# One more SBUF buffer, fewer early reloads, paired loads and split tiles at the turn between two passes of a channel-attention kernel

## The chip, the cores and the metric

The kernel runs on one core of one Trainium2 chip. The metric is the device time of one execution in microseconds (us). Two executions (one of an experiment, one of the kernel before) took over 770 us; they were left out as slow, from medians too. The experiments e9, e10 and e11 ran on another chip than the other experiments; their ratios are against the kernel before on that chip (757.38 us there).

## The reference

```python
def setup_inputs():                       # H = W = C = 384, k = 1, everything bf16
    return {"x": normal(1, 384, 384, 384) * 0.05, "w1d": normal(1) * 0.05}

def reference(x, w1d):
    g = x.sum over all pixels / (H * W)    # one mean per channel
    s = sigmoid(g * w1d[0])                # k = 1: no neighbours
    return x * s                           # per channel
```

No output can be written until every input has been read, because `s` needs the mean over all pixels. The input has 113.25 MB in 72 tiles. It does not fit in SBUF, the memory on the chip, where a build with 18 tiles was refused (see "The change"), so most of it must be read twice.

## The kernel before

In this kernel PE does the matmuls (2.77 us for a tile in the trace), DVE the multiplies (3.35 us) and ACT the sigmoid (0.58 us); SP issues the loads of the tiles and ACT their stores.

The input is cut into 72 tiles of 128 partitions x 12 KB (1.57 MB). In the first pass, SP loads every tile into a ring of 16 buffers, and PE multiplies it by a matrix of ones into one PSUM accumulator, which gives the channel sums in all partitions. ACT applies the sigmoid. In the second pass, DVE multiplies tiles by `s` in place and ACT's queue stores them. The last tiles are still in SBUF and need no second load. Each other tile is reloaded into a buffer whose store is done. `NS` tiles of those still in SBUF are given up on purpose: their buffers take reloads before any store is done, so these reloads run while PE, ACT and DVE finish the first pass.

```python
TILE_BYTES_TARGET = 12 * 1024
MAX_BUF_BYTES = 192 * 1024
MAX_BUFS = 16
NS_TARGET = 3
...
    resident = list(range(NT - NBUF, NT - NS))                            # kept: 13 tiles
    reload = list(range(0, NT - NBUF)) + list(range(NT - NS, NT))         # read twice: 59 tiles
    vorder = resident + reload
...                                                                       # sync engine
            for i in range(NT):                                           # first pass
                b = i % NBUF
                j = i // NBUF
                if j > 0:
                    sync.wait_ge(pe_sems[b], j)
                sync.dma_start(bufs[b][:], x_tiles[i]).then_inc(in_sems[b], 16)
            for i in reload:                                              # second pass
                b = p2_buf[i]
                sync.wait_ge(pe_sems[b], cnt1[b])
                if load_wait_out[i] > 0:                                  # 0 for the first NS of them
                    sync.wait_ge(out_sems[b], load_wait_out[i])
                sync.dma_start(bufs[b][:], x_tiles[i]).then_inc(in_sems[b], 16)
```

## Time and profile before

| | kernel before |
|---|---|
| median, lowest, highest of its first 6 runs | 757.33, 755.71, 758.18 us |
| span of the profiled run | 753.9 us |
| tiles moved: first loads + reloads + stores | 72 + 59 + 72 = 203 |
| bytes moved | 319.48 MB |
| busy: PE, DVE | 27%, 32% |

The first view is from the profile page of the kernel before: the span in 40 equal slices, with the busy share in tenths of PE, DVE and the DMA engines, and then the rate in GB/s.

```profile
PE   5777777777777740000000000000000000000000
...
DVE  0000000000000029998445354444535444453300
...
DMA  8999999999999999999999999999999999999998
GB/s 341 425 426 425 423 426 424 426 422 426 424 425 423 426 395 424 429 429 430 431 430 430 428 432 430 428 429 431 431 429 430 430 431 429 429 429 431 432 430 382
```

DMA is at 90% or more in nearly every slice. PE works in the first 15 slices, DVE in the rest, and neither is full for long. So the DMA engines bound the kernel. The table of DMA queues (packets, MB, share of the time of 16 engines) says what they carry; q1 is the load queue and q10 the store queue:

```profile
q1 hardware_dynamic: 18864, 206.05, 64.8%
q10 hardware_dynamic: 10368, 113.25, 35.3%
```

The next view gives the DMA issues by group: how many, KB each, median us from issue to landing.

```profile
buf<-in_x_dram SPq DMA_DIRECT2D x131, 1536.0 KB, 27.0
out_dram<-buf ACTq DMA_DIRECT2D x72, 1536.0 KB, 71.0
```

A store lands 71 us after its issue (the median).

This is the timeline of the kernel before (start us, length us, engine, line, operation, output<-inputs, count, and in brackets the idle time before it):

```profile
268.47 8.56 SPq L152 DMA_DIRECT2D buf<-in_x_dram  x3
...
273.90 2.77 PE L186 MATMUL acc<-buf,ones_mat 128*128 128x384 bf16 x16 [1.76 <-DMA buf<-in_x_dram]
276.78 0.58 ACT L123 ACTIVATE s_bc<-acc,w_scaled 128x384 bf16<-128x384 f32 x1 [274.54 <-PE acc L186]
277.39 6.63 DVE L172 TENSOR_TENSOR buf<-buf,s_bc 128x6144 bf16<-128x6144 bf16 x2 [266.04 <-ACT s_bc L123]
280.78 0.38 ACTq L133 DMA_DIRECT2D out_dram<-buf  x1
```

The last tile is seen by PE at 273.90. The first store is issued at 280.78, 6.88 us later: 16 matmuls, the sigmoid, one multiply of 3.35 us. The early reloads were issued from 268.47 on. Now the DMA engines in chosen windows of the same run (window, length, busy time of PE, PEld (PE's weight loads), DVE, ACT, POOL with counts, then the granted TensorE clock, DMA share, GB/s):

```profile
10.00:255.00 245.00, 183.20 (x1053) 97.67 (x1052) 0.15 (x1) 0.00 (x0) 0.00 (x0) 1.00 1.01 425
270.00:273.00 3.00, 2.14 (x14) 1.07 (x11) 0.00 (x0) 0.00 (x0) 0.00 (x0) 1.00 0.95 385
273.00:276.00 3.00, 2.10 (x13) 1.28 (x14) 0.00 (x0) 0.00 (x0) 0.00 (x0) 1.00 0.99 385
276.00:279.00 3.00, 0.68 (x5) 0.20 (x2) 1.61 (x1) 0.58 (x1) 0.00 (x0) 1.00 1.02 369
279.00:282.00 3.00, 0.00 (x0) 0.00 (x0) 3.00 (x2) 0.00 (x0) 0.00 (x0) 0.91 0.93 373
380.00:680.00 300.00, 0.00 (x0) 0.00 (x0) 137.70 (x41) 0.00 (x0) 0.00 (x0) 0.50 1.01 430
```

The rate is 425 GB/s in the first pass and 430 in the steady second pass, so a tile costs about 3.7 us anywhere. Around the turn the rate dips, but DMA is hardly idle (shares of 0.93 to 1.02): three early reloads fill the turn.

### The profile page before, as it was taken

The page shows a single profiled execution, that of the slowest core. Times are in us where ns is not written, and L with a number is a line of the kernel's source. Part 1 is how long each engine was busy: PE and PEld are TensorE (multiplying, and loading weights), DVE is VectorE, ACT ScalarE, POOL GpSimd, SP SyncE. Part 2 cuts the span into 40 slices and gives each one's busy share as a digit, 9 for nine tenths or more (in the row PEclk, how much of TensorE's full clock was granted, in tenths as well). Part 3 has the DMA queues.
Part 4 walks back from the last instruction along what each step waited for, and adds up shares of the span by engine and source line. Part 5 has one row for each costly group of instructions (what it writes and reads, how often), then busy time and mean ns, then how long its engine had stood idle before and what let it go on. Part 6 is the DMA issues. An engine that isn't in the chain of part 4 may idle for free.

```text
span 753.9 us, 2681 instructions
## 1 busy us (share of the span) xinstructions
PE 201.7 (27%) x1152; PEld 107.5 (14%) x1152; DVE 240.2 (32%) x74; ACT 2.1 (0%) x3; POOL 1.0 (0%) x6
## 2 busy tenths in 40 slices
PE   5777777777777740000000000000000000000000
PEld 2343333343444420000000000000000000000000
DVE  0000000000000029998445354444535444453300
ACT  0000000000000000000000000000000000000000
POOL 0000000000000000000000000000000000000000
PEclk9999999999999995555555555555555555555555
DMA  8999999999999999999999999999999999999998
GB/s 341 425 426 425 423 426 424 426 422 426 424 425 423 426 395 424 429 429 430 431 430 430 428 432 430 428 429 431 431 429 430 430 431 429 429 429 431 432 430 382
DMA packets 29388, 319.48 MB, mean 424 GB/s; under 512 B 3392, under 2 KB 3392, under 8 KB 3392
## 3 DMA queue, kind: packets, MB, share of 16 engines
q1 hardware_dynamic: 18864, 206.05, 64.8%
q10 hardware_dynamic: 10368, 113.25, 35.3%
q8 instruction: 9, 0.15, 0.1%
q0 software_dynamic: 144, 0.00, 0.0%
q14 instruction: 3, 0.02, 0.0%
HBM read 206.05 MB, written 113.25 MB: 424 GB/s over the span
## 4 chain that ended last, share of the span: by engine, by line
another core or an unknown queue 40%; SPq 32%; DMA 14%; DVE 6%; issue 1%; PE 0%; ACT 0%; ACTq 0%
SPq L146 30%; DMA buf<-in_x_dram 8%; DMA out_dram<-buf 6%; DVE buf L172 6%; SPq L152 2%; PE acc L186 0%; SPq L151 0%; ACT s_bc L123 0%; ACTq L122 0%
## 5 line engine op out<-in xcount | busy, mean ns | idle before, releaser
L172 DVE TENSOR_TENSOR buf<-buf,s_bc 128x6144 bf16<-128x6144 bf16 x72 | 239.8, 3356 | 457.0 <-ACT s_bc L123 266.0
L186 PE MATMUL acc<-buf,ones_mat 128*128 128x384 bf16 x1152 | 201.7, 329 | 74.9 <-DMA buf<-in_x_dram 74.9
L186 PEld LDWEIGHTS acc<-buf,ones_mat 128*128 128x128 bf16 x1152 | 107.5, 98 | 168.8 <-DMA buf<-in_x_dram 94.6
L158 DVE TENSOR_SCALAR w_scaled<-w_f 128x1 f32<-128x1 f32 x1 | 0.2, 154 | 10.2 <-DMA w_f<-in_w1d_dram 10.2
L123 ACT ACTIVATE s_bc<-acc,w_scaled 128x384 bf16<-128x384 f32 x1 | 0.6, 581 | 274.5 <-PE acc L186 274.5
L118 ACT ACT_TABLE_LOAD x1 | 1.3, 1283 | 0.7 <-PEq L208 0.7
L112 POOL DMA_DIRECT2D w_f<-in_w1d_dram x1 | 0.7, 652 | 0.8 <-POOLq L208 0.8
L156 DVE MEMSET ones_mat<- 128x128 bf16 x1 | 0.2, 165 | 0.8 <-PEq L208 0.8
L118 ACT ACTIVATE warm<-warm 128x1 f32<-128x1 f32 x1 | 0.2, 203 | 0.0
L113 POOL MEMSET warm<- 128x1 f32 x1 | 0.1, 118 | 0.0
L208 POOL MEMSET const-uint8-127<- 128x1 uint8 x1 | 0.1, 101 | 0.0
L208 POOL MEMSET const-float32-0.0<- 128x1 f32 x1 | 0.1, 98 | 0.2 <-issue 0.2
L208 POOL MEMSET const-float32-1.0<- 128x1 f32 x1 | 0.1, 98 | 0.0
L208 POOL MEMSET const-bfloat16-1.0<- 128x1 bf16 x1 | 0.1, 98 | 0.0
## 6 DMA issues: line engine op xcount, KB each, us to landing
buf<-in_x_dram SPq DMA_DIRECT2D x131, 1536.0 KB, 27.0
out_dram<-buf ACTq DMA_DIRECT2D x72, 1536.0 KB, 71.0
w_f<-in_w1d_dram POOLq DMA_DIRECT2D x1, 0.5 KB, 10.0
```

The source lines that it names most:

```text
L112: gpsimd.dma_start(w_f32[:], w_bcast_src).then_inc(w_sem, 16)
L113: gpsimd.memset(warm[:, 0:1], 0.0).then_inc(warm_sem, 1)
L118: scalar.activation(warm[:, 1:2], warm[:, 0:1], mybir.ActivationFunctionType.Sigmoid)
L123: scalar.activation(s_bc[:], acc[:, :C], mybir.ActivationFunctionType.Sigmoid, scale=w_scaled[:, 0:1],).then_inc(s_sem, 1)
L146: sync.dma_start(bufs[b][:], x_tiles[i]).then_inc(in_sems[b], 16)
L152: sync.dma_start(bufs[b][:], x_tiles[i]).then_inc(in_sems[b], 16)
L156: vector.memset(ones_mat[:], 1.0).then_inc(ones_sem, 1)
L158: vector.tensor_scalar_mul(w_scaled[:], w_f32[:], inv_hw).then_inc(wsc_sem, 1)
L172: vector.tensor_tensor(bv, bv, s_b, mybir.AluOpType.mult).then_inc(vec_sems[b], 1)
L186: ins = tensor.matmul(acc[:, :C], ones_mat[:], bufs[b][:, t * C : (t + 1) * C], start=first, stop=last,)
L208: nc = _bacc.Bacc("TRN2", target_bir_lowering=False, num_devices=1)
```

## The change

It aims to move fewer bytes and to shorten the turn. It has four parts.

1. 17 buffers (204 KB per partition) instead of 16, in one array, so one tile more stays in SBUF. A version with 18 (216 KB) failed to build.
2. `NS` from 3 to 1. Together with part 1, reloads fall from 59 to 56.
3. The first pass loads pairs of neighbouring tiles with one DMA. The DRAM layout puts the two tiles side by side in a partition, so a run has 24 KB.
4. The last load comes in four quarters, each with its own semaphore, and the first six resident tiles are multiplied and stored in halves.

```diff
-MAX_BUF_BYTES = 192 * 1024
-MAX_BUFS = 16
-NS_TARGET = 3
+MAX_BUF_BYTES = 204 * 1024
+MAX_BUFS = 32
+NS_TARGET = 1
+GROUP = 2
...
+    RS = NT - MG - NS
+    recycled = list(range(RS, RS + NS))
+    resident = [i for i in range(NT - NBUF, NT) if i not in recycled]
+    reload = list(range(0, NT - NBUF)) + recycled
...
-    x_tiles = x.flatten_outer_dims().rearrange("(n p t) c -> n p (t c)", p=P, t=T)
+    x_mt = x.flatten_outer_dims().rearrange("(n p t) c -> n p (t c)", p=P, t=MG * T)
...                                                     # grouping of the first loads
+            i % MG == 0
+            and g < MG
+            and i + g < NT - 2 * MG
+            and (i + g) % NBUF == (i % NBUF) + g
...
+    HALF = 6
+    split = set(resident[:HALF])
...                                                     # sync engine, the last load
+                if gi == NT - 1:
+                    F4 = FD // LQ                       # LQ = 4
+                    for q in range(LQ):
+                        sync.dma_start(
+                            slot(s0)[:, q * F4 : (q + 1) * F4],
+                            dram_tiles(x_mt, gi, 1)[:, q * F4 : (q + 1) * F4],
+                        ).then_inc(last_sems[q], 16)
+                    continue
+                sync.dma_start(slot(s0, g), dram_tiles(x_mt, gi, g)).then_inc(
+                    in_sems[s0], 16
+                )
...                                                     # vector engine (stores are split the same way)
+                if i in split:
+                    for h in range(2):
+                        ...
+                        vector.tensor_tensor(
+                            bh, bh, s_h, mybir.AluOpType.mult
+                        ).then_inc(vec_sems[b], 1)
+                    continue
```

More of the change, by code (lines that the diff above doesn't have):

```diff
@@ L38, in bass_standalone__channel_attn_eca__vision_kernel @@
     assert C <= 512, "channel count must fit one PSUM bank"
+    MG = GROUP if (rows_pp % (GROUP * T) == 0 and NT >= GROUP) else 1
     NBUF = max(1, min(MAX_BUFS, NT, MAX_BUF_BYTES // tile_pp_bytes))
-    NS = 0 if NT <= NBUF else min(NS_TARGET, NBUF)
-    resident = list(range(NT - NBUF, NT - NS))
-    reload = list(range(0, NT - NBUF)) + list(range(NT - NS, NT))
+    NS = 0 if NT <= NBUF else min(NS_TARGET, NBUF - MG)
+    RS = NT - MG - NS
+    if RS < NT - NBUF:
+        RS = NT - NBUF
+    recycled = list(range(RS, RS + NS))
+    resident = [i for i in range(NT - NBUF, NT) if i not in recycled]
+    reload = list(range(0, NT - NBUF)) + recycled
     assert sorted(resident + reload) == list(range(NT))
@@ L47, in bass_standalone__channel_attn_eca__vision_kernel, with dram_tiles @@
     inv_hw = 1.0 / float(H * W)
-    x_tiles = x.flatten_outer_dims().rearrange("(n p t) c -> n p (t c)", p=P, t=T)
-    o_tiles = out.flatten_outer_dims().rearrange("(n p t) c -> n p (t c)", p=P, t=T)
+    x_mt = x.flatten_outer_dims().rearrange("(n p t) c -> n p (t c)", p=P, t=MG * T)
+    o_mt = out.flatten_outer_dims().rearrange("(n p t) c -> n p (t c)", p=P, t=MG * T)
+    def dram_tiles(view, i, g):
+        n, q = divmod(i, MG)
+        assert q + g <= MG
+        return view[n][:, q * FD : (q + g) * FD]
     w_bcast_src = bass.AP(w1d.tensor, w1d.offset, [[0, P], [1, 1]])
+    arena = nc.alloc_sbuf_tensor("arena", [P, NBUF * FD], x.dtype)
     ones_mat = nc.alloc_sbuf_tensor("ones_mat", [P, P], x.dtype)
@@ L63, in bass_standalone__channel_attn_eca__vision_kernel @@
     s_sem = nc.alloc_semaphore("s_sem")
-    bufs = []
+    LQ = 4
+    last_sems = [nc.alloc_semaphore(f"last_sem{q}") for q in range(LQ)]
     in_sems, pe_sems, vec_sems, out_sems = [], [], [], []
     for b in range(NBUF):
-        bufs.append(nc.alloc_sbuf_tensor(f"buf{b}", [P, FD], x.dtype))
         in_sems.append(nc.alloc_semaphore(f"in_sem{b}"))
@@ L71, in bass_standalone__channel_attn_eca__vision_kernel, with slot @@
         out_sems.append(nc.alloc_semaphore(f"out_sem{b}"))
-    cnt1 = [len(range(b, NT, NBUF)) for b in range(NBUF)]
-    buf_of_last = {i: i % NBUF for i in range(NT - NBUF, NT)}
-    p2_buf = {}
+    def slot(b, n=1):
+        return arena[:, b * FD : (b + n) * FD]
+    groups = []
+    i = 0
+    while i < NT:
+        g = 1
+        while (
+            i % MG == 0
+            and g < MG
+            and i + g < NT - 2 * MG
+            and (i + g) % NBUF == (i % NBUF) + g
+        ):
+            g += 1
+        groups.append((i, g))
+        i += g
@@ new lines, in bass_standalone__channel_attn_eca__vision_kernel @@
+    cnt1 = [len(range(b, NT, NBUF)) for b in range(NBUF)]
+    p1_wait = {}
+    dma_cnt = [0] * NBUF
+    p1_loads = []
+    uses1 = [0] * NBUF
+    for gi, g in groups:
+        s0 = gi % NBUF
+        waits = []
+        for q in range(g):
+            s = s0 + q
+            if uses1[s] > 0:
+                waits.append((s, uses1[s]))
+            uses1[s] += 1
+        if gi != NT - 1:
+            dma_cnt[s0] += 1
+        for q in range(g):
+            p1_wait[gi + q] = (s0, 16 * dma_cnt[s0])
+        p1_loads.append((waits, s0, gi, g))
@@ L76, in bass_standalone__channel_attn_eca__vision_kernel @@
+    slot_of_tail = {i: i % NBUF for i in range(NT - NBUF, NT)}
+    p2_slot = {}
     for i in resident:
-        p2_buf[i] = buf_of_last[i]
+        p2_slot[i] = slot_of_tail[i]
     for m, i in enumerate(reload):
         if m < NS:
-            p2_buf[i] = buf_of_last[NT - NS + m]
+            p2_slot[i] = slot_of_tail[recycled[m]]
         else:
-            p2_buf[i] = p2_buf[vorder[m - NS]]
-    n_loads = list(cnt1)
+            p2_slot[i] = p2_slot[vorder[m - NS]]
+    proc_index = {}
     n_proc = [0] * NBUF
-    load_wait_out = {}
@@ L86, in bass_standalone__channel_attn_eca__vision_kernel @@
-    vec_wait = {}
-    store_wait_vec = {}
-    proc_index = {}
     for i in vorder:
-        b = p2_buf[i]
+        b = p2_slot[i]
         proc_index[i] = n_proc[b]
         n_proc[b] += 1
-    load_wait_in_value = {}
-    for m, i in enumerate(reload):
-        b = p2_buf[i]
-        n_loads[b] += 1
-        load_wait_in_value[i] = 16 * n_loads[b]
-        load_wait_out[i] = 16 * proc_index[i]
-    for i in vorder:
-        b = p2_buf[i]
-        if i in load_wait_in_value:
-            vec_wait[i] = ("in", load_wait_in_value[i])
-        else:
-            vec_wait[i] = ("pe", cnt1[b])
-        store_wait_vec[i] = proc_index[i] + 1
@@ L106, in bass_standalone__channel_attn_eca__vision_kernel @@
-    total_stores = list(n_proc)
+    vec_wait = {}
+    load_wait_out = {}
+    for i in reload:
+        b = p2_slot[i]
+        dma_cnt[b] += 1
+        vec_wait[i] = ("in", 16 * dma_cnt[b])
+        load_wait_out[i] = 16 * proc_index[i]
+    for i in resident:
+        vec_wait[i] = ("pe", cnt1[p2_slot[i]])
+    HALF = 6
+    split = set(resident[:HALF])
+    xtra = [0] * NBUF
+    for i in split:
+        assert proc_index[i] == 0
+        xtra[p2_slot[i]] = 1
+    store_wait_vec = {i: proc_index[i] + 1 + xtra[p2_slot[i]] for i in vorder}
@@ L108, in bass_standalone__channel_attn_eca__vision_kernel @@
+    for i in reload:
+        if proc_index[i] > 0:
+            load_wait_out[i] += 16 * xtra[p2_slot[i]]
+    F2 = FD // 2
     with nc.Block() as block:
@@ L121, in _ @@
             scalar.wait_ge(wsc_sem, 1)
-            scalar.wait_ge(pe_sems[(NT - 1) % NBUF], cnt1[(NT - 1) % NBUF])
+            last_slot = (NT - 1) % NBUF
+            scalar.wait_ge(pe_sems[last_slot], cnt1[last_slot])
             scalar.activation(
@@ L130, in _ @@
             for i in vorder:
-                b = p2_buf[i]
+                b = p2_slot[i]
+                if i in split:
+                    for h in range(2):
+                        scalar.wait_ge(vec_sems[b], h + 1)
+                        scalar.dma_start(
+                            dram_tiles(o_mt, i, 1)[:, h * F2 : (h + 1) * F2],
+                            slot(b)[:, h * F2 : (h + 1) * F2],
+                        ).then_inc(out_sems[b], 16)
+                    n_st[b] += 2
+                    continue
                 scalar.wait_ge(vec_sems[b], store_wait_vec[i])
-                scalar.dma_start(o_tiles[i], bufs[b][:]).then_inc(out_sems[b], 16)
+                scalar.dma_start(dram_tiles(o_mt, i, 1), slot(b)).then_inc(
+                    out_sems[b], 16
+                )
                 n_st[b] += 1
@@ L140, in _ @@
         def _(sync):
-            for i in range(NT):
-                b = i % NBUF
-                j = i // NBUF
-                if j > 0:
-                    sync.wait_ge(pe_sems[b], j)
-                sync.dma_start(bufs[b][:], x_tiles[i]).then_inc(in_sems[b], 16)
+            for waits, s0, gi, g in p1_loads:
+                for s, val in waits:
+                    sync.wait_ge(pe_sems[s], val)
+                if gi == NT - 1:
[8 more added lines that the diff above has]
+                    in_sems[s0], 16
+                )
             for i in reload:
-                b = p2_buf[i]
+                b = p2_slot[i]
                 sync.wait_ge(pe_sems[b], cnt1[b])
@@ L151, in _ @@
                     sync.wait_ge(out_sems[b], load_wait_out[i])
-                sync.dma_start(bufs[b][:], x_tiles[i]).then_inc(in_sems[b], 16)
+                sync.dma_start(slot(b), dram_tiles(x_mt, i, 1)).then_inc(
+                    in_sems[b], 16
+                )
         @block.vector
@@ L161, in _ @@
             for i in vorder:
-                b = p2_buf[i]
+                b = p2_slot[i]
                 if first:
@@ L170, in _ @@
                     vector.wait_ge(pe_sems[b], val)
-                bv = bufs[b][:].rearrange("p (t c) -> p t c", t=T)
+                if i in split:
+                    s_h = s_bc[:].unsqueeze(1).broadcast_to([P, T // 2, C])
+                    for h in range(2):
+                        bh = slot(b)[:, h * F2 : (h + 1) * F2].rearrange(
+                            "p (t c) -> p t c", t=T // 2
+                        )
+                        vector.tensor_tensor(
+                            bh, bh, s_h, mybir.AluOpType.mult
+                        ).then_inc(vec_sems[b], 1)
+                    continue
+                bv = slot(b).rearrange("p (t c) -> p t c", t=T)
                 vector.tensor_tensor(bv, bv, s_b, mybir.AluOpType.mult).then_inc(
@@ L180, in _ @@
                 b = i % NBUF
-                j = i // NBUF
-                tensor.wait_ge(in_sems[b], 16 * (j + 1))
+                s0, val = p1_wait[i]
+                if b == s0 and i != NT - 1:
+                    tensor.wait_ge(in_sems[s0], val)
                 for t in range(T):
+                    if i == NT - 1 and t % (T // LQ) == 0:
+                        tensor.wait_ge(last_sems[t // (T // LQ)], 16)
                     first = i == 0 and t == 0
@@ L188, in _ @@
                         ones_mat[:],
-                        bufs[b][:, t * C : (t + 1) * C],
+                        slot(b)[:, t * C : (t + 1) * C],
                         start=first,
```

## The prediction

> **What bounds it now.** DMA traffic. The page's slice rows show the mean busy share of the DMA engines at 90% or more in 38 of 40 slices, at 341 to 432 GB/s. The table of queues gives 319.48 MB over a 753.9 us span. PE is busy 27% and DVE 32%. Reading stretches by window: 425 GB/s while the first pass only loads (10 to 265 us), 430 GB/s while loads and stores mix (390 to 690 us), so one 1.57 MB tile costs about 3.7 us of all DMA engines wherever it stands. Before moves 203 tiles: 72 loads, 59 reloads, 72 stores.
>
> **What changes.**
> 1. Pool 17 instead of 16 buffers, and one recycled tile instead of three: reloads fall from 59 to 56, total 200 tiles. Saved: 4.72 MB, 3 x 3.68 = 11.0 us, all on the critical resource.
> 2. Turnaround between the passes. Before (timeline): last tile's matmuls start at 273.90, ACT 276.78, first DVE multiply 277.39 (3.35 us), first store issued 280.78, that is 6.9 us after the landing. From the first load (issued 0.74, data at full rate from about 2.5, consumed at 7.66) I estimate 1.7 us from issue to data and 1.3 us from last data to the consumer. Three reloads (11 us) cover this completely; the windows of 273 to 283 us show dips but no idle DMA. After: the last load in quarters leaves 4 matmuls (0.8 us), ACT 0.6, half a multiply 1.7, so the store is issued about 3.3 us after landing and its data comes at about 4.9. The single reload covers only to about 2.4. I expect a hole of about 2.5 us, a cost.
> 3. Pairs of tiles loaded with 24 KB runs (32 pairs). A clean 12 KB packet takes 460 ns in the trace's packet records (466 in the first pass). [...] If runs stay whole, 32 x 8 packets per engine x 8 ns, plus 32 semaphore writes of 9 ns: 2.3 us saved. The 6 KB and 3 KB pieces of the split stores and last load give 0.6 us back. Net -1.7 us, uncertain: runs may be cut, and the new 24 KB pitch of single tiles may change HBM behaviour either way.
> 4. One reload ahead instead of three: harmless in steady state, because about 14 stores stay queued and keep the DMA engines busy. DVE waits, the split multiplies and PE waits for pairs are off the critical path.
>
> **Sum.** -11.0 + 2.5 - 1.7 = -10.2 us: 747 us, range 743.5 to 752. Chances: faster by over 2% (below 742.2) 0.10; within 2% 0.88; slower 0.02.
>
> **What would show it.** Queues: load queue about 201.3 MB, total 314.8 MB. Windows around the end of the first pass: one short stretch of low DMA share, 1 to 4 us, between the single reload and the first store. Issue of the first store about 3.3 us after the last landing. First pass rate 425 to 429 GB/s. Mixed rate still 430. Landing time of stores rises above 71 us (deeper store backlog), landing time of reloads falls below 17 us. Last slices unchanged.
>
> **What would make it wrong.** If the single reload ahead lets the store queue run dry, or the mixed rate falls below 427 GB/s, it gains nothing. If the 24 KB pitch costs HBM efficiency (1% is 7 us), the gain shrinks to a few us; if 24 KB runs remove the 466 against 460 ns of the first pass as well, 3 us more. If the hole is fully covered, 744.5.

The passage cut from part 3 derived the 8 ns per packet from a figure that no trace of the kernel before shows. The packet records of the changed kernel show the 8 ns: two packets of 12 KB take 2 x 460 = 920 ns, one of 24 KB 912 ns. What part 3 says of the 24 KB pitch and of runs that may be cut were open questions, which e5, e6 and e8 below answer.

## The result

| | before | changed |
|---|---|---|
| median, lowest, highest | 757.44, 755.71, 759.51 us (16 runs) | 746.14, 745.88, 746.60 us (8 runs) |
| span of the profiled run | 753.9 us | 744.3 us |

The ratio is 0.9851, with a 95% interval of 0.9841 to 0.9862. A ratio here is the mean time of one kernel's fast runs over that of the other's fast runs of the same rounds, so it is not quite the ratio of the medians. The change gains 11.3 us, 1.5%: within 2%, and inside the range. The profiled run of the kernel before was the fastest of its 16, so the two traces differ by 9.6 us, less than the medians do.

The page of the changed kernel, DMA share and rate in 40 slices:

```profile
DMA  8999999999999989999999999999999999999998
GB/s 350 430 429 433 425 433 428 429 435 424 433 429 425 426 340 391 422 430 432 428 431 431 429 429 431 431 429 430 431 429 429 431 429 430 431 431 427 432 430 374
```

The queues of the changed kernel, load queue first:

```profile
q1 hardware_dynamic: 14256, 201.33, 63.7%
q10 hardware_dynamic: 11232, 113.25, 35.9%
```

The load queue carries 201.33 MB, three tiles less, as forecast. The first pass shows several slices of 428 to 435 GB/s where the kernel before had 422 to 426. One slice stands out with 340 GB/s: the turn. Its timeline in the changed kernel:

```profile
265.04 0.33 SPq L221 DMA_DIRECT2D arena<-in_x_dram  x1
...
269.87 1.79 PE L270 MATMUL acc<-arena,ones_mat 128*128 128x384 bf16 x8 [0.15 <-DMA arena<-in_x_dram]
270.83 0.44 PEld L270 LDWEIGHTS acc<-arena,ones_mat 128*128 128x128 bf16 x4 [0.53 <-DMA arena<-in_x_dram]
271.76 0.58 ACT L173 ACTIVATE s_bc<-acc,w_scaled 128x384 bf16<-128x384 f32 x1 [269.52 <-PE acc L270]
272.37 3.43 DVE L248 TENSOR_TENSOR arena<-arena,s_bc 128x3072 bf16<-128x3072 bf16 x2 [257.37 <-ACT s_bc L173]
274.16 0.38 ACTq L185 DMA_DIRECT2D out_dram<-arena  x1
```

PE sees the last quarter at 270.83, which is 3.07 us earlier than before. The first store goes out at 274.16, 3.33 us after that, instead of 6.88. The windows show the price:

```profile
10.00:255.00 245.00, 185.48 (x1060) 103.92 (x1061) 0.15 (x1) 0.00 (x0) 0.00 (x0) 0.97 1.00 428
270.00:273.00 3.00, 1.51 (x8) 0.51 (x6) 0.63 (x1) 0.58 (x1) 0.00 (x0) 1.00 0.52 219
273.00:276.00 3.00, 0.00 (x0) 0.00 (x0) 3.00 (x3) 0.00 (x0) 0.00 (x0) 1.00 0.35 145
276.00:279.00 3.00, 0.00 (x0) 0.00 (x0) 3.00 (x2) 0.00 (x0) 0.00 (x0) 0.62 1.03 416
279.00:282.00 3.00, 0.00 (x0) 0.00 (x0) 3.00 (x3) 0.00 (x0) 0.00 (x0) 0.50 1.07 354
380.00:680.00 300.00, 0.00 (x0) 0.00 (x0) 137.31 (x41) 0.00 (x0) 0.00 (x0) 0.50 1.01 430
```

In the two windows from 270 to 276 us the DMA share is 0.52 and 0.35. The single early reload is done and no store is there yet. The steady rate is 430 GB/s, as before. The issues by group:

```profile
out_dram<-arena ACTq DMA_DIRECT2D x66, 1536.0 KB, 71.6
...
arena<-in_x_dram SPq DMA_DIRECT2D x63, 1536.0 KB, 12.3
```

Reloads land sooner (the 63 single loads have a median of 12.3 us; those of the second pass had 17.2 us before and have 12.3 us now). The stores still land after 71.6 us.

The DMA packet records of the two traces close the account. I integrated busy time over the 16 engines and divided by the 1.0086 to which it sums in a full stretch; "hole" is the idle time in the 12 us before the first store's data, "slow packets" the excess over clean packets in the 30 us after it (a clean packet takes the commonest time of its size; semaphore writes of 9 ns, packets of 4 bytes, 16 to each transfer, are counted with them), "ragged end" the mean idle time of the engines in the last 10 us. All are times averaged over the 16 engines.

| us | before | changed | difference |
|---|---|---|---|
| PE sees the last load | 273.90 | 270.83 | -3.07 |
| from there to the first store's issue | 6.88 | 3.33 | -3.55 |
| from there to its first data | 1.90 | 0.88 | -1.02 |
| first to last store data | 470.42 | 467.87 | -2.55 |
| in that stretch: clean packets | 468.70 | 464.96 | -3.74 |
| in that stretch: slow packets | 0.33 | 1.65 | +1.32 |
| in that stretch: ragged end | 1.01 | 0.83 | -0.18 |
| hole before the first store's data | 0.20 | 3.18 | +2.98 |

The first four lines add up to -10.19 us at the last byte. The spans differ by 0.5 us less, because 1.35 us follow the last byte in the changed kernel and 0.83 us did before. The hole is no further term of this sum: it is idle time inside the first three lines.

### The profile page after: what moved, and what is told of

Its sections match the earlier page's. It is cut to its first block, busy times and chain, and to the rows that moved or that the text cites. A ratio compares the mean times of both kernels' runs of the same rounds, so it can differ in the third digit from the quotient of the medians.

```text
span 744.3 us, 2684 instructions
## 1 busy us (share of the span) xinstructions
PE 201.4 (27%) x1152; PEld 112.5 (15%) x1152; DVE 240.2 (32%) x80; ACT 2.1 (0%) x3; POOL 1.0 (0%) x6
## 3 DMA queue, kind: packets, MB, share of 16 engines
q1 hardware_dynamic: 14256, 201.33, 63.7%
HBM read 201.33 MB, written 113.25 MB: 423 GB/s over the span
## 4 chain that ended last, share of the span: by engine, by line
another core or an unknown queue 45%; DMA 19%; PE 17%; DVE 6%; SPq 5%; issue 0%; ACT 0%; ACTq 0%
PE acc L270 17%; DMA arena<-in_x_dram 13%; DMA out_dram<-arena 6%; DVE arena L253 3%; SPq L208 3%; DVE arena L248 3%; SPq L221 2%; SPq L213 0%; SPq L220 0%; ACT s_bc L173 0%; ACTq L172 0%
## 5 line engine op out<-in xcount | busy, mean ns | idle before, releaser
L253 DVE TENSOR_TENSOR arena<-arena,s_bc 128x6144 bf16<-128x6144 bf16 x66 | 219.9, 3357 | 178.7 <-DMA arena<-in_x_dram 178.7
L270 PE MATMUL acc<-arena,ones_mat 128*128 128x384 bf16 x1152 | 201.4, 335 | 70.3 <-DMA arena<-in_x_dram 70.2
L270 PEld LDWEIGHTS acc<-arena,ones_mat 128*128 128x128 bf16 x1152 | 112.5, 100 | 158.7 <-DMA arena<-in_x_dram 71.3
L248 DVE TENSOR_TENSOR arena<-arena,s_bc 128x3072 bf16<-128x3072 bf16 x12 | 20.1, 1754 | 257.4 <-ACT s_bc L173 257.4
## 6 DMA issues: line engine op xcount, KB each, us to landing
out_dram<-arena ACTq DMA_DIRECT2D x66, 1536.0 KB, 71.6
arena<-in_x_dram SPq DMA_DIRECT2D x63, 1536.0 KB, 12.3
```

The costliest lines, as they stand in the source:

```text
L248: vector.tensor_tensor(bh, bh, s_h, mybir.AluOpType.mult).then_inc(vec_sems[b], 1)
L253: vector.tensor_tensor(bv, bv, s_b, mybir.AluOpType.mult).then_inc(vec_sems[b], 1)
L270: ins = tensor.matmul(acc[:, :C], ones_mat[:], slot(b)[:, t * C : (t + 1) * C], start=first, stop=last,)
```

## The experiments

Two ways to count were at stake. Theory B is the bookkeeping of the prediction: every tile not moved is worth 3.7 us, and the hole is a cost of its own. Theory A says that the turn is a gap of fixed length in which only early reloads can run. Then an early reload that fits in the gap is neither a gain nor a loss, and only what overfills the gap costs time. Every kernel gave the correct result. Each was run in 5 rounds beside the kernel before; "ratio" is against that.

### Early reloads: none, two, three

```diff
-NS_TARGET = 1
+NS_TARGET = 0        # e1;  2 in e9, 3 in e2
```

> The changed kernel with no recycled tile (0 reloads issued early instead of 1; 199 tiles moved instead of 200). Theory A, the turnaround is a fixed gap of about 6.9 us that DMA cannot use for anything but an early reload: the saved reload only widens the hole from about 3.2 to 6.9 us, time stays at 746 us (745 to 747). Theory B, the one the prediction was written in, every tile not moved is worth 3.7 us and the hole is a separate fixed cost of 2.5 to 3 us: 742.4 us.

> The changed kernel with two recycled tiles. The run without recycled tiles shows a hole of about 7.1 us in DMA traffic, so two early reloads (7.4 us) should just fill it: 746.1 + 0.3 = 746.4 us, no hole left. If each reload costs 3.7 us whatever the hole: 749.8 us. With three recycled tiles 749.95 us were measured, so the step from two to three should be the full 3.5 to 3.7 us.

> The changed kernel with three recycled tiles, as before (202 tiles moved). Theory A: early reloads fill the turnaround of 6.9 us and then 11.1 - 6.9 = 4.2 us too much: 750.3 us, no hole in the windows. Theory B: two more tiles at 3.7 us each with the hole unchanged: 753.5 us.

| early reloads | tiles moved | median us | ratio | hole, us | slow packets, us | ragged end, us |
|---|---|---|---|---|---|---|
| 0 (e1) | 199 | 746.12 | 0.9857 | 6.93 | 1.82 | 0.67 |
| 1 (changed) | 200 | 746.14 | 0.9851 | 3.18 | 1.65 | 0.83 |
| 2 (e9) | 201 | 748.03 (746.43 to 749.29) | 0.9875 | 0.10 | 1.47 | 2.55 |
| 3 (e2) | 202 | 749.95 | 0.9909 | -0.05 | 0.29 | 1.70 |

DMA windows of the run without early reloads (e1), columns as before:

```profile
269.00:272.00 3.00, 2.51 (x14) 0.96 (x12) 0.00 (x0) 0.17 (x1) 0.00 (x0) 1.00 0.03 12
272.00:275.00 3.00, 0.00 (x0) 0.00 (x0) 2.56 (x2) 0.41 (x1) 0.00 (x0) 1.00 0.00 0
```

And windows of the run with two (e9):

```profile
270.00:273.00 3.00, 1.48 (x8) 0.50 (x6) 0.65 (x1) 0.58 (x1) 0.00 (x0) 1.00 1.01 428
273.00:276.00 3.00, 0.00 (x0) 0.00 (x0) 3.00 (x3) 0.00 (x0) 0.00 (x0) 1.00 0.92 387
```

Moving one tile less (e1) saved nothing: the hole grew by 3.75 us, which is just the tile. Theory B, which asked for 742.4 us, falls. With two the hole is filled (shares of 1.01 and 0.92), and with three the time is 3.8 us above the changed kernel, against 4.2 expected. The steps were missed: from one to two it is 1.9 us instead of 0.3, and from two to three 1.9 us instead of 3.5 to 3.7. In the trace with two, 1.7 us more lie at the ragged end, where some DMA engines finish before others; its runs also scatter over 2.9 us, and the interval of its ratio (0.9858 to 0.9891) just overlaps that of the changed kernel. With three, the slow packets after the turn are nearly absent, which makes the second step smaller. So theory A holds for the sum and for the hole, but the steps are blurred by 1 to 2 us of effects that I did not separate.

### Early reloads in the kernel before

```diff
-NS_TARGET = 3        # in the kernel before
+NS_TARGET = 1
```

> The kernel before with one recycled tile instead of three and nothing else changed: 4.7 MB x 2/3 = 3.1 MB less traffic. Theory A: its turnaround is 3.55 us longer than the changed kernel's, so about 10.6 us, which three reloads (11.1 us) fill almost exactly; taking two away gives only 0.5 us, 756.8 us, and leaves a hole of about 7 us. Bytes alone: 757.3 - 7.4 = 749.9 us.

The median was 756.51 us against 757.38, ratio 0.9993 (0.9979 to 1.0006): no resolved difference, although two tiles less were moved. Bytes alone would have given 749.9 us. The windows of this run:

```profile
270.00:273.00 3.00, 1.75 (x11) 0.84 (x9) 0.00 (x0) 0.00 (x0) 0.00 (x0) 1.00 0.32 131
273.00:276.00 3.00, 2.22 (x14) 1.38 (x15) 0.00 (x0) 0.00 (x0) 0.00 (x0) 1.00 0.00 0
276.00:279.00 3.00, 0.55 (x4) 0.10 (x2) 1.73 (x1) 0.58 (x1) 0.00 (x0) 1.00 0.48 111
```

Here is the hole, 6.80 us by the packet records. In the old kernel the turn was long enough to hide three reloads, so cutting them alone was worth almost nothing. In the changed kernel the same cut, from three to one, is worth 3.8 us. There the turn is shorter, 3.33 instead of 6.88 us from the last load to the first store's issue, and the next experiment shows that the split tiles shortened it. Three early reloads without the splits were not run in the changed kernel, so that the splits alone make the difference is argued and not shown.

### The splits undone

```diff
-    LQ = 4
+    LQ = 1
...
-    HALF = 6
+    HALF = 0
```

> The changed kernel with the last load in one piece and the first six multiplies and stores whole. Turnaround longer by 12 matmuls (about 2.0 us) and half a multiply (1.6 us), less 0.5 us for the small pieces: 749.2 us, first store issued about 6.9 us after the last landing, hole about 6.5 us. A rival for whom the turnaround is hidden by the queues: 745.5 to 746 us.

The median was 749.14 us (ratio 0.9906), 3.0 us more than the changed kernel. The timeline of this run:

```profile
270.68 2.77 PE L270 MATMUL acc<-arena,ones_mat 128*128 128x384 bf16 x16 [2.07 <-DMA arena<-in_x_dram]
...
277.56 0.37 ACTq L192 DMA_DIRECT2D out_dram<-arena  x1
```

From 270.68 to 277.56 are 6.88 us, exactly the old length of this chain, and the hole is 6.63 us. The turn is on the critical path and the split tiles take 3.0 us off it net. The quarters of the last load were not undone by themselves.

```diff
-    HALF = 6
+    HALF = 1
```

> The changed kernel with only the first resident tile split in halves instead of six. My estimate: 5 tiles fewer in 6 KB runs, 5 x 8 x 8 ns per engine = 0.3 us less, 745.8 us; if the slow packets after the first stores (about 1.5 us in excess of clean ones in the 15 us after the hole) come from the half tiles, 744.6 us; if halves are needed beyond the first tile to keep the DMA fed, 747 us or more.

The 8 ns of this estimate are those of the packet records of the changed kernel (two packets of 6 KB take 2 x 234 = 468 ns, one of 12 KB 460). The median of the four fast runs was 747.2 us (ratio 0.9879), 1.1 us more than the changed kernel; the fifth run was slow. The four scatter from 746.82 to 750.02 us, so the size is loose. The guess of 745.8 missed; the outcome named for the case that more halves are needed, 747 or more, is the one that came. This run's windows show why:

```profile
278.00:279.00 1.00, 0.00 (x0) 0.00 (x0) 1.00 (x1) 0.00 (x0) 0.00 (x0) 0.50 0.85 338
279.00:280.00 1.00, 0.00 (x0) 0.00 (x0) 1.00 (x2) 0.00 (x0) 0.00 (x0) 0.50 0.15 61
```

A second hole opens at 279 to 280 us. The first two half stores are done before DVE has finished the next whole multiply (a whole one takes 3.35 us). DVE makes a tile only a little faster than DMA stores one (3.35 against about 3.7 us), so the backlog grows slowly, and more than one split tile is needed. The slow packets did not vanish either (1.25 us), nor without any split (e4: 1.97 us). So half tiles are not their cause.

### The 17th buffer undone

```diff
-MAX_BUF_BYTES = 204 * 1024
+MAX_BUF_BYTES = 192 * 1024
```

> The changed kernel with 16 buffers instead of 17 (201 tiles moved, hole as in the changed kernel). Both theories: one more tile, 749.8 us. A rival for whom the gain is all in the turnaround and the first pass, and the buffer is worth nothing: 746 us.

The median was 749.68 us (ratio 0.9904), 3.5 us more: the price of one tile.

### Pairs and pitch

```diff
-            and g < MG       # e5: keep the layout, load single tiles
+            and g < 1
```

```diff
-GROUP = 2                    # e6: old layout, single tiles; the recycled tile and the
+GROUP = 1                    # last single loads kept as in the changed kernel
...
-    RS = NT - MG - NS
+    RS = NT - 2 - NS
...
-            and i + g < NT - 2 * MG
+            and i + g < NT - 4
```

> The changed kernel with its DRAM layout (a partition holds two tiles side by side, 24 KB pitch) but every load of the first pass single, in 12 KB runs. If the first pass gained by longer runs alone: the first pass ends about 3 us later, near 273.9 us in the trace, and the time is 749.1 us. If the layout gave the gain: 746 us.

> The changed kernel with the old DRAM layout (12 KB pitch) and single loads; everything else as changed. Same time as the run with the pitch alone, 749.1 us, if the pitch costs nothing; 7 us apart from it if the pitch costs or gives 1% of HBM efficiency.

The medians were 748.85 and 749.35 us (ratios 0.9893 and 0.9899, intervals that overlap). The first pass of e5, in the same window as shown above of the kernels before and changed:

```profile
10.00:255.00 245.00, 183.85 (x1057) 98.05 (x1055) 0.15 (x1) 0.00 (x0) 0.00 (x0) 1.00 1.01 426
```

The first pass of e6:

```profile
10.00:255.00 245.00, 185.36 (x1057) 98.81 (x1056) 0.15 (x1) 0.00 (x0) 0.00 (x0) 0.99 1.01 426
```

Both load at 426 GB/s, against 428 with pairs over the same window. In the packet records of e5 the data of the last load ended at 272.63 us, 2.3 us later than in the changed kernel (270.34), where about 3 were expected. The pitch has no visible effect. The pairs are worth 2.7 to 3.2 us.

```diff
-GROUP = 2
+GROUP = 4
```

> The changed kernel with groups of four tiles (48 KB runs where the slots allow) in the first pass. If the cost is some 8 ns per run: a packet record of 49152 bytes at about 1816 ns against 912 for 24576 and 460 for 12288, and about 0.7 us gained, 745.4 us; if runs over 24 KB are cut, no change of packet size, 746.1 us; coarser recycling of 17 slots may cost instead.

The median was 747.49 us (ratio 0.9877), 1.4 us worse than pairs, where 0.7 us of gain were estimated. The packet sizes did what was expected. Clean packet times, the commonest value in the packet records of all runs:

```
run in bytes   3072   6144   12288   24576   49152
ns              121    234     460     912    1815
```

These lie on one line within 1 ns: 8 ns, and 452 ns for every 12 KB. 17 buffers do not divide into groups of four: in the stretch from 20 to 240 us of the span there were 984 packets of 12 KB, against 512 in the changed kernel, so more of the loads were single. Still the loading did not suffer: in the packet records the data of the last quarter ended at 269.58 us, against 270.34 in the changed kernel, close to the gain estimated. PE lost it again. This is its work at the end of the first pass in e8:

```profile
239.71 33.06 PE L270 MATMUL acc<-arena,ones_mat 128*128 128x384 bf16 x192 [3.96 <-DMA arena<-in_x_dram]
```

PE had waited 3.96 us for a group of four tiles, got all four at once, and then worked through 192 matmuls, the last 12 tiles, without a break until 272.77 us, 3.2 us after the last data. At 2.75 us a tile it could not catch up in time with loads that came every 3.7 us. ACT started 1.1 us later (272.87 against 271.76), and the hole grew to 4.8 us. Here longer runs paid only as far as PE kept up with them.

### A version that beats both

It has no early reload. The first two resident tiles go in quarters, the third in halves. From the sixth resident tile on, stores and reloads go in pairs with 24 KB runs. A reload waits for the stores of its own pair of slots. The core of the edit:

```diff
+    PARTS = {0: 4, 1: 4, 2: 2}  # pieces of the first resident tiles
+    SINGLE = 5                  # resident tiles stored one by one before stores go in pairs
+    units = [(tail[0],)] + [(i, i + 1) for i in tail[1::2]]
...
+        if not done:            # second-pass stores of resident pairs
+            stores.append(([(s0 + q, nvec[s0 + q]) for q in range(len(u))], u[0], len(u), s0, 0, len(u) * FD))
...
+            for waits, i, g, s0 in reloads:
+                for sl, v in waits:
+                    sync.wait_ge(out_sems[sl], v)
+                sync.dma_start(slot(s0, g), dram_tiles(x_mt, i, g)).then_inc(
+                    in_sems[s0], 16
+                )
```

> An improved version: no recycled tile, first two resident tiles multiplied and stored in quarters, the third in halves, and from the sixth resident tile on all stores and reloads of the second pass in pairs with 24 KB runs. Estimate from the packet records (460 ns per 12 KB, 912 per 24 KB, 9 per semaphore write): 120 tile moves x (8 x 4 + 4.5) ns = 4.4 us less, and 0.85 us less turnaround for a quarter instead of a half multiply: 741 us. If coarser recycling in pairs starves the DMA engines, no gain or a loss.

The median was 742.40 us (741.99 to 743.00), ratio 0.9803 (0.9790 to 0.9817): 2% faster than the kernel before, though the interval leaves open on which side of 2%, and 3.7 us faster than the changed one. The estimate was 741. Its window in the steady second pass:

```profile
380.00:680.00 300.00, 0.00 (x0) 0.00 (x0) 134.43 (x41) 0.00 (x0) 0.00 (x0) 0.50 1.00 432
```

The first store's data came at 274.31 instead of 275.04 us, 0.73 us earlier, where 0.85 were expected. The mixed rate rose from 430 to 432 GB/s, which gave 2.7 us from first to last store data instead of the 4.4 us estimated. The estimate summed packet times, but the records overlap: in a full stretch they sum to 1.0086 of the time with 12 KB runs and to 1.0046 with 24 KB runs, about 4 ns per packet. So about half of the 8 ns per run is covered by this overlap.

## Why the prediction was right

The time was 746.1 us against 747 predicted. Point by point:

- **DMA bounds the kernel, 3.7 us per tile.** Right. The load queue carries 201.33 MB as forecast, and the 17th buffer by itself is worth 3.5 us.
- **The turn.** The first store was forecast 3.3 us after the last landing and came after 3.33. The hole was forecast at 2.5 us and is 3.18. The estimate of 1.7 us from issue to data was too high for idle DMA engines (0.88 us, from the start of the first store's issue at 274.16 to its data at 275.04; with early reloads queued ahead it was 1.90 us, before).
- **The pairs.** The sign was right, the term too small. The first pass ended 3.07 us earlier, where pairs and pieces together were put at 1.7. The estimate priced the 8 ns per run only. The overlap just named hides about half of that. The rest is that fewer packets were slow: from 20 to 260 us of the span, in the first pass, the excess over clean packets was 3.05 us per engine before, 2.21 in e5 (single loads, otherwise as changed) and 1.16 with pairs. The prediction had named this as a possible extra. The step from 3.05 to 2.21 came without pairs and is not the pitch (e6, with the old layout, has 2.20); what caused it was not tested.
- **One early reload instead of three is harmless in the steady state.** Right: 430 GB/s in both. The "about 14 stores" of the forecast are in the traces: from 400 to 680 us, 13 or 14 tiles were multiplied and not yet stored before, 14 or 15 in the changed kernel.
- **Landing times.** Reloads fell from 17.2 to 12.3 us, as said. Stores were expected to rise above 71 us and hardly moved (71.0 before, 71.6 now). ACT's issue instruction itself took 0.34 to 0.38 us for the first 17 stores before and the first 22 in the changed kernel, and later mostly 6.36 us in both (6.36 is the median of all stores before, and of the whole ones in the changed kernel). From 400 to 680 us, 8 to 11 stores were issued and not landed in both, near the 71.6 / 7.3 = 10 that one store per two tile times gives. I read this as a limit on the stores outstanding, so that a deeper backlog waits in ACT and not in the measured landing. That reading was not tested.
- **Not foreseen: 1.3 us of slow packets after the turn.** They offset part of the gain. They appear in every run with a hole, and in the run with two early reloads, and hardly in the two with three (before and e2). Their cause stays open.

That the sum came so close is partly luck: against the forecast the end of the first pass gained about 1.4 us more, while the hole cost 0.7 us more and the slow packets 1.3 us that were not foreseen.

The sum was right, but its split was not the useful one. Counting "three tiles less, plus a hole" gives the right total, yet it suggests that dropping the last early reload would pay another 3.7 us, and e1 shows that it pays nothing. Taken one at a time out of the changed kernel, the parts are worth 3.5 us (buffer), 2.7 to 3.2 us (pairs), 3.0 us (splits) and 3.8 us (early reloads). That sums to about 13 us, more than the 11.3 us of the whole. One reason that the runs show is that the last two depend on each other: in the old kernel dropping two early reloads gained at most 1.6 us (the lower end of the interval of e10).

## What to carry to other kernels

In a kernel bound by DMA, look for the moments when the DMA queue has nothing it may do, and cost them as gaps of time. Here a transfer that fitted in such a gap was free, and removing it gained nothing (746.12 us in e1 against 746.14) as long as the gap itself was not shorter. Shorten the chain that closes the gap by splitting its first and last pieces (3.0 us here), and keep splitting until a backlog exists (with one split tile, e7, the DMA share fell to 0.15 in a second hole). Make runs longer where buffers allow (2.7 to 3.2 us for the pairs), but check that the engine that uses the tiles still finishes with the last load (in e8 PE ended 3.2 us after the last data).
